# Local and pooled attention in front of a gated MLP: the first six pairs in a short form, weight bits shifted in SBUF, and a new stored order

## The chip, the cores and the metric

The kernel runs on one core of a Trainium2 chip. Its time is device time in microseconds (us). The engines are named as the profile names them: PE (TensorE, matmuls) with PEld (its weight loads), DVE (VectorE), ACT (ScalarE), POOL (GpSimd) and SP (SyncE, which here only starts transfers).

## The reference

For 8 batches and 8 heads, with 576 positions and 64 channels a head, the reference adds two attentions, and passes the joined heads (512 channels) through a gated MLP:

```python
q_d, k_d, v_d = (mean over groups of 4 positions of q, k, v)      # 144 positions
out_up = np.repeat(sm_attn(q_d, k_d, v_d), 4, axis=2)
mask = np.abs(pos[:, None] - pos[None, :]) < 4
scores = np.where(mask, scale * q @ k.T, -1e9)
attn = softmax(scores)                                            # a band of 7
x = out_up + attn @ v                                             # heads joined
h = gelu(x @ w_in); u, v = halves of h                            # 512 -> 1024
v_n = (v - mean) / sqrt(var + 1e-6) * g_ln
gated = u * (w_sg @ v_n + b_sg)                                   # w_sg is 576 x 576
out = x + gated @ w_out
```

All inputs are fp32.

## The kernel before

**Pairs.** Two heads fill the 128 partitions, so there are 32 pairs, g = 0 to 31, four to a batch. Everything is kept transposed (channels or keys on partitions). After the four pairs of a batch comes its MLP. The program is a list of tasks, each with a short name and the pair's number behind it. For a pair:

- `lq`, `lk`, `lv`, `lw` load q, k, v for the pooled part (four rows side by side) and v for the local part; `qs`, `ks`, `vs` sum four neighbours of q, k and v.
- `S` makes the local scores in two PSUM banks (ten tiles of 64 queries by 64 keys: four in one bank, six in the other), `Y` the pooled scores; `YS` is both at once. Of the local tiles only a band counts, so a mask (0 or a large negative number) is added.
- `mx` and `my` take the maxima of rows, `nx` and `ny` make from them the bias of an exponential, `ea` and `eb` are the exponentials of the local tiles (one instruction for each of the ten, since each has a bias of its own; it also gives the sum of its row), `ec` those of the pooled scores; `re` and `rc` make reciprocals, `np` and `nq` normalise.
- `T`, `U`, `t` turn the probabilities with matmuls, `pa`, `pb`, `pc`, `pe` copy them from PSUM; `D` is the product with v, first the pooled part, then the local one; `oe`, `od`, `xa`, `xb` merge both, `xh`, `xl`, `xc` split the result into a high and a low part.

The MLP works on those parts in fp32r, with three products for one (high by high, high by low, low by high): `v` (L691), `u` and `s` and `o` (all L769), with tasks `vg` to `vl`, `ua`, `sa`, `sm`, `gh`, `gl`, `oa` and the store `os` around them.

**Weights.** The weights w_in and w_out come as fp64 words, 512 KB for each of 12 blocks (y0 to y3 for v, z0 to z3 for u, r0 to r3 for o). For each block VectorE or ScalarE scales the high word (`wq`), VectorE shifts its bits into place in two operations (`wb`, L309 and L311; the first writes PSUM), ScalarE scales the low word (`wu`), GpSimd adds (`wt`), and `wh` and `wl` split it into the high and the low part.

**The first four pairs** go another way (`EARLY_S, EARLY_D = 4, 4`). Their mask is added by two matmuls of the identity with the mask ahead of the scores (L417, fp32), and the exponentials read PSUM; the other pairs add the mask on VectorE while copying to SBUF (`ma`, `mb`, L432). And their pooled v is not summed: `D` takes each of the four rows by itself, with 64 pooled matmuls in place of 16 (L573; the local ones are L589).

**What sets the order.** The stored text `ORDER` lists every task once, with the engine behind a slash where there is a choice (`/A`, `/V`, `/P`, for loads `/A` or `/S` is the queue). The program emits the tasks in that order and nothing reorders them later: each engine's queue is the order of its tasks in the text. `place` gives each task its buffer, from 8 PSUM banks and pools of 10 (`X`) and 38 (`R`) SBUF buffers:

```python
SIZES = {"ps": 8, "X": 10, "R": 38}
    order, spots = place(tasks, SIZES)
    with tc.manual_schedule():
        for t, e in order:
            t.emit(e)
```

The mask, the identity, the two turning matrices and g_ln are one array, `small_sb` (463 KB), which SP's queue loads second.

Of the kernel before, what the change touches and what calls it, by code (L numbers as in the profile page):

```python
# [7 lines left out]
F32 = mybir.dt.float32  # L8
# [7 lines left out]
P = 128  # L16
# [72 lines left out]
wy0 lk0/A lq0/A lq1/A small ks0/P wqy0/A wuy0 wby0 wty0 wy3 qs0/V S0 mx0 lw1/A qs1/P nx0/V ea0 why0/V wqy3/V Y0 my0  # L89
lk1/S ks1/P wy1 wuy3 wby3 wqy1/V ny0/A ec0 wly0/P wby1 wty3 wuy1 wty1 wy2 wqy2/A S1 wuy2 wby2 Y1 my1 wty2 lq3 wz2 eb0  # L90
mx1 re0/A rc0 ny1/A ec1 nx1/A ea1 nq0/P lk3 np0/P lk2 wuz2 S3 lq2 S2 wz3 wqz2/V wbz2 mx3 qs3/V lq4 mx2 eb1 wqz3/A T0
pa0/V why3/V U0 t0 pb0/A lv0/S lw0/S nx2/A pc0/V pe0/V ks2/P qs2/P Y2 my2 re1/A rc1 ks3/P ny2/V D0 ea2 eb2 wbz3 qs4/V
wz1 np1/P oe0/V ec2 re2/A nq1/P lk4 ks4/P lv1/S wtz2 od0 xa0 xb0 T1 pa1/A t1 U1 pb1/V pc1/V pe1/A nx3/A Y3 my3 ea3 rc2
np2/P nq2/P wqz1/A ny3/A YS4 xh0/V ma4 mb4 my4 mx4 eb3 ec3 wz0 D1 xl0/P lv2 wbz1 nx4/V T2 lw2 lq5 U2 re3/V oe1/A
wly3/P rc3 np3/P lk5 whz2/A wlz2/P t2 pa2/A wqz0/A pb2/V pc2/V wq3 vk3.0 pe2/A qs5/V ny4/A ec4 D2 wr0 od1 xa1 wuz0
nq3/P wbz0 eb4 T3 vk1.0 lv4 lv3 oe2/V od2 ks5/P xa2 xb2 xb1 lw3 pa3/A wq1 lk6 t3 U3 pb3/V pc3/V wr3 xh1/V why1/A
wly1/V YS5 pe3/A D3 ma5 my5 ea4 re4/A rc4 nq4/V wuz3 lw4 t4 oe3/V wtz0 xl1/P vk3.1 why2/A wly2/P mb5 wr1 xh2/A xl2/V
ks6/V ny5/A mx5 ec5 b lq6 od3 xa3 xb3 xh3/V np4/P xc0 wqr0/A lv5 wur0 wtz3 vk0.0 vk0.1 wq2 xc2 wqr1/A xl3/V nx5/A
# [890 lines left out]
```

## Time and profile before

| | before |
|---|---|
| median of 3 runs | 589.13 us (587.82 to 589.57) |
| span of the profiled execution | 585.7 us |
| PE busy | 559.7 us (96%) |
| PEld busy | 522.2 us (89%) |
| DVE busy | 432.7 us (74%) |
| ACT busy | 354.0 us (60%) |
| POOL busy | 306.2 us (52%) |
| DMA | 63.21 MB, mean 108 GB/s |

The profile shows one execution, from its first instruction to its last (the span); of the profiled execution no other time is given than this span. Shares of busy time are means over the whole span. In what follows, a row of a timeline has a start, a length and the instruction, with the idle time before it and what ended it in brackets; a row of a chain has a start, a length and the work, and "issue" there is time in which an engine waited for nothing that the profile shows; a group of instructions has its line, engine, operation, output and inputs with shape and type, count, then busy us and mean ns, and the idle us before them.

### The profile page before, as it was taken

How to read it: one execution, taken by the hardware profiler on the slowest of the kernel's cores; microseconds unless marked ns; L12 is line 12 of the kernel's file. 1: busy time of each engine (PE TensorE's matmuls, PEld its weight loads, DVE VectorE, ACT ScalarE, POOL GpSimd, SP SyncE). 2: the span in 40 equal slices, each digit the busy share in tenths (PEclk: the TensorE clock that was granted, in tenths of full speed). 3: DMA queues.
4: the chain of work that ended last, by engine and by line, in shares of the span. 5: the costliest groups of instructions: out<-in, count | busy, mean ns of one | idle time of the engine just before them, and what ended most of it. 6: DMA issues, size and time to landing. Idle time of an engine off the chain costs nothing.

```text
span 585.7 us, 17441 instructions
## 1 busy us (share of the span) xinstructions
PE 559.7 (96%) x6992; PEld 522.2 (89%) x6992; DVE 432.7 (74%) x947; ACT 354.0 (60%) x1227; POOL 306.2 (52%) x384
## 2 busy tenths in 40 slices
PE   4778999999999999999999999999999999999997
PEld 2567799988998999989999899988999899998997
DVE  3957998968795998886658786777668877652662
ACT  2958997859868758476656583195833879301300
POOL 4866769674856432461475753554434653820440
PEclk9879999999999999999999999999999999999999
DMA  8999014534503321242046052241117430300103
GB/s 318 305 281 286 14 48 128 158 118 137 144 26 98 97 83 58 96 157 63 16 134 193 13 194 90 59 134 42 37 62 230 118 100 1 113 1 1 41 2 121
DMA packets 30610, 63.21 MB, mean 108 GB/s; under 512 B 3520, under 2 KB 3776, under 8 KB 30528
## 3 DMA queue, kind: packets, MB, share of 16 engines
q1 hardware_dynamic: 29952, 60.86, 33.3%
q8 instruction: 55, 0.90, 0.7%
q10 hardware_dynamic: 576, 1.23, 0.6%
q14 instruction: 27, 0.22, 0.1%
HBM read 52.64 MB, written 9.44 MB: 106 GB/s over the span
## 4 chain that ended last, share of the span: by engine, by line
PE 81%; DVE 8%; ACT 5%; issue 3%; DMA 1%; POOL 0%; SPq 0%; ACTq 0%; DVEq 0%; POOLq 0%
PE ps L769 49%; PE ps L691 15%; PE ps L573 4%; ACT X L484 3%; PE ps L512 3%; PE ps L589 3%; PE ps L424 2%; PE ps L445 2%; PE ps L521 2%; DMA small_sb<-in_small_dram 1%; ACT pd L492 1%; DVE R L740 1%; DVE wsg_l L352 1%; DVE st L721 1%; ACT L492 1%
## 5 line engine op out<-in xcount | busy, mean ns | idle before, releaser
L769 PE MATMUL ps<-wsg_h,R 128*128 128x288 f32 x576 | 120.8, 297 | 0.0
L769 PE MATMUL ps<-R,weight_r 128*128 128x288 f32 x768 | 109.4, 297 | 0.3 <-ACT pd L492 0.3
L769 PE MATMUL ps<-X,weight_z 128*128 128x288 f32 x512 | 108.2, 296 | 0.3 <-DVE X L432 0.3
L769 PEld LDWEIGHTS ps<-R,weight_r 128*128 128x128 f32 x768 | 103.8, 188 | 2.1 <-DVE R L826 0.4
L691 PE MATMUL ps<-weight_y,X 128*128 128x512 f32 x320 | 98.0, 400 | 0.1
L484 ACT ACTIVATE X<-X,nb 128x64 f32<-128x64 f32 x280 | 93.5, 338 | 3.2 <-DVE nb L463 2.8
L769 PEld LDWEIGHTS ps<-wsg_h,R 128*128 128x128 f32 x576 | 94.2, 188 | 0.2
L769 PE MATMUL ps<-wsg_l,R 128*128 128x288 f32 x320 | 92.8, 296 | 0.4 <-DVE wsg_l L352 0.4
L769 PEld LDWEIGHTS ps<-X,weight_z 128*128 128x128 f32 x512 | 83.9, 188 | 1.2 <-ACT weight_z L221 0.7
L769 PE MATMUL ps<-R,weight_z 128*128 128x288 f32 x256 | 75.4, 295 | 0.0
L691 PEld LDWEIGHTS ps<-weight_y,X 128*128 128x128 f32 x320 | 58.2, 189 | 12.5 <-POOL X L221 0.4
L769 PEld LDWEIGHTS ps<-wsg_l,R 128*128 128x128 f32 x320 | 60.2, 188 | 0.6 <-DVE wsg_l L352 0.6
L732 POOL TENSOR_TENSOR rs<-rs,nhalf 128x1 f32<-128x1 f32 (+1 forms) x40 | 24.5, 614 | 63.0 <-DVE rs L723 62.9
L807 DVE SCALAR_TENSOR_TENSOR vs<-ps,small_sb,b_sb 128x288 f32<-128x288 f32 x64 | 32.4, 513 | 32.6 <-PE ps L769 31.6
L484 ACT ACTIVATION_READ_ACCUMULATOR X<-X,nb 128x1 f32 x280 | 53.1, 190 | 0.0
L691 PE MATMUL ps<-weight_y,R 128*128 128x512 f32 x128 | 50.7, 396 | 0.0
L408 POOL TENSOR_TENSOR pairs<-R 112x256 f32<-112x256 f32 x56 | 44.6, 796 | 10.2 <-DMA R<-in_v_dram 10.2
L788 ACT ACTIVATE R<-ps 128x288 f32<-128x288 f32 x64 | 24.7, 411 | 40.9 <-PE ps L769 40.8
L221 ACT CAST R<-R 128x512 fp32r<-128x512 f32 (+2 forms) x44 | 28.0, 641 | 34.0 <-DVE R L814 14.2
L769 PEld LDWEIGHTS ps<-R,weight_z 128*128 128x128 f32 x256 | 48.1, 188 | 0.3
L826 POOL TENSOR_TENSOR R<-R,R 128x576 fp32r<-128x576 f32 x21 | 31.1, 1484 | 28.6 <-PE ps L521 14.4
L814 POOL TENSOR_TENSOR R<-R,vs 128x288 f32<-128x288 f32 x23 | 20.4, 894 | 45.2 <-DVE vs L807 39.2
(111 smaller groups left out, 1210.7 us busy)
## 6 DMA issues: line engine op xcount, KB each, us to landing
R<-in_v_dram SPq DMA_DIRECT2D x56, 224.0 KB, 3.2
X<-in_vw_dram SPq DMA_DIRECT2D x31, 320.0 KB, 4.8
R<-in_kT_dram SPq DMA_DIRECT2D x31, 293.0 KB, 3.8
out_dram<-R SPq DMA_DIRECT2D x31, 288.0 KB, 3.3
R<-in_qT_dram SPq DMA_DIRECT2D x30, 293.0 KB, 4.4
weight_y<-in_w_in_dram SPq DMA_DIRECT2D x4, 512.0 KB, 8.9
weight_z<-in_w_in_dram SPq DMA_DIRECT2D x4, 512.0 KB, 7.9
weight_r<-in_w_out_dram SPq DMA_DIRECT2D x4, 512.0 KB, 6.0
```

The costliest lines, as they stand in the source:

```text
L221: (nc.scalar.copy if e == "A" else ENG[e].tensor_copy)(**kw)
L408: ENG[e].tensor_tensor(out=pairs, in0=v[:, 0:2], in1=v[:, 2:4], op=ALU.add)
L484: nc.scalar.activation(out=st["ms"][:, t, :], in_=src, func=AF.Exp, bias=st["nb"][:, t:t + 1], scale=scale, accum_out=sums[par][:, t:t + 1])
L512: nc.tensor.matmul(out=out, lhsT=st["ms"][0:LD, 2 * c:2 * c + 2, :], rhs=turn_l, is_transpose=True, start=True, stop=True)
L573: nc.tensor.matmul(out=out, lhsT=lhsT, rhs=pdt[ks, probs, h * QC:(h + 1) * QC], start=first, stop=last)
L691: nc.tensor.matmul(out=acc, lhsT=r32(l), rhs=r32(weights[f"y{k}"][:, 0, w]), start=(i == 0 and ks[0] == 0), stop=(i == len(ops) - 1 and ks ...
L732: nc.gpsimd.tensor_tensor(out=rs[0:n], in0=rs[0:n], in1=nhalf[0:n], op=ALU.pow)
L769: nc.tensor.matmul(out=acc[:, 0:HALF], lhsT=r32(l), rhs=r32(r), start=(first and n == 0), stop=(last and n == len(ops) - 1))
L788: nc.scalar.activation(out=us[i // 2][:, half(i)], in_=at["ps", "m", b, "u", i][:, 0:HALF], func=AF.Gelu_apprx_tanh)
L807: nc.vector.scalar_tensor_tensor(out=vsb[i], in0=at["ps", "m", b, "s", i][:, 0:HALF], scalar=g_sb[:, i // 2:i // 2 + 1], in1=b_sb[:, half( ...
L814: ENG[e].tensor_tensor(out=u[:, half(i)], in0=u[:, half(i)], in1=vsb[i], op=ALU.mult)
L826: ENG[e].tensor_tensor(out=r32(gl[d]), in0=us[d], in1=gh[d], op=ALU.subtract)
```

## The change

- **Six pairs, not four, in the short form** (`EARLY, DIRECT = 6, 0`). The mask matmul is now in fp32r: GpSimd rounds the mask and the identity once into a buffer (task `early`). Mask and identity are both stored with the sign turned, so their product is the same.
- **The maximum is taken off in PSUM.** A new task `B` (`below`) multiplies minus the identity with the row maxima, each spread over 64 columns, and adds that to the scores in both banks (two fp32 matmuls). With no bias left that differs from tile to tile, `ea` is one exponential for each bank (128x256 and 128x384), with no sum; `sr`, a VectorE reduction, makes the sums. `nx` and `eb` fall away for these pairs.
- **Pooled v is summed for every pair** (`vs`, on GpSimd or now also VectorE), and `D` has 16 pooled matmuls everywhere. The first four pairs load whole rows of v for it, 0.46 MB where it was 0.39.
- **The shift `wb` stays in SBUF**: the first operation writes the block's SBUF buffer, the second works there in place. It takes no PSUM bank any more.
- **`small_sb` is split** into `early_sb` (mask and minus identity, 295 KB, first on ScalarE's queue) and a smaller `small_sb` (0.18 MB, fifth on SP's).
- **`ORDER` is new from beginning to end**, with other choices of engines: of `pc` 23 of 32 are on ScalarE (before 14), of `xh` 21 (9), of `pb` 20 (15), of `gh` 15 (19); of `xl` 23 are on GpSimd (15), of `qs` 19 (13), of `np` 21 (17); of `vs` 12 are on VectorE (0).

```diff
 ORDER = """
-wy0 lk0/A lq0/A lq1/A small ks0/P wqy0/A wuy0 wby0 wty0 wy3 qs0/V S0 mx0 lw1/A qs1/P nx0/V ea0 why0/V wqy3/V Y0 my0
...
+lq0/S mask/A early/P wy2 lk0/A S0 qs0/P ks0/V Y0 mx0 wqy2/A wby2 wuy2 lv1/A lq1/S qs1/V my0 lk1/S ks1/P small/S B0 ea0
...
         def shift(e):
-            bits, done, hw = like(buf(*keys[1])).bitcast(I32), like(buf(*keys[0])).bitcast(I32), word(1)
-            nc.vector.tensor_scalar(out=bits, in0=hw.bitcast(I32), scalar1=3,
+            done, hw = like(buf(*key)).bitcast(I32), word(1)
+            nc.vector.tensor_scalar(out=done, in0=hw.bitcast(I32), scalar1=3,
                                     scalar2=0x7FFFFFF8, op0=ALU.logical_shift_left, op1=ALU.bitwise_and)
-            nc.vector.scalar_tensor_tensor(out=done, in0=hw.bitcast(I32), scalar=-0x80000000, in1=bits,
+            nc.vector.scalar_tensor_tensor(out=done, in0=hw.bitcast(I32), scalar=-0x80000000, in1=done,
                                            op0=ALU.bitwise_and, op1=ALU.bitwise_or)
...
+        def below(e):
+            for i in range(2):
+                top = bc_last(stats[par][:, i * NA:i * NA + NW[i]], KB)
+                nc.tensor.matmul(out=spv(i), lhsT=minus_sb, rhs=top, start=False, stop=True, skip_group_check=True)
...
+        def exp_early(e):
+            st["ms"] = buf("X", "ms", g).rearrange("p (t k) -> p t k", k=KB)
+            for i in range(2):
+                nc.scalar.activation(out=st["ms"][:, i * NA:i * NA + NW[i]], in_=spv(i), func=AF.Exp, scale=scale)
+
+        def sum_early(e):
+            nc.vector.tensor_reduce(out=sums[par][:, 0:NT], in_=st["ms"], axis=AX.X, op=ALU.add)
...
+            add(N("mx"), {"V": 0.95}, top, [SN(), last_nx])
+            add(N("B"), {"T": 1.2}, below, [N("mx")])
+            add(N("ea"), {"A": 0.75}, exp_early, [N("B")], takes=[("X", "ms", g)],
+                gives=[("ps", "s", g, 0), ("ps", "s", g, 1)], func="e")
+            add(N("sr"), {"V": 0.8}, sum_early, [N("ea"), N("rc", 2)])
```

The rows below are instructions in the order of an engine's queue: line, operation, output and inputs, shape. PE at the very beginning, pair 0, before (mask, scores, then pooled scores; `ps` is a PSUM bank):

```order
L417 MATMUL ps_135<-small_sb 128x256
L417 MATMUL ps_136<-small_sb 128x384
L424 MATMUL ps_135<-R_115,R_117 64x64 x2
L424 MATMUL ps_136<-R_115,R_117 64x64 x2
...
L424 MATMUL ps_136<-R_115,R_117 64x64 x6
L445 MATMUL ps_175<-kd_83,qd_75 64x144 x2
L445 MATMUL ps_176<-kd_83,qd_75 64x144 x2
```

And after (L424 is the mask matmul, L431 the scores, L457 the pooled scores, L438 is `B`; the last two rows are pair 1's pooled scores):

```order
L424 MATMUL ps_123<-R_117 128x256
L424 MATMUL ps_124<-R_117 128x384
L431 MATMUL ps_123<-R_121,R_114 64x64 x2
L431 MATMUL ps_124<-R_121,R_114 64x64 x2
...
L431 MATMUL ps_124<-R_121,R_114 64x64 x6
L457 MATMUL ps_151<-kd_84,qd_76 64x144 x2
L457 MATMUL ps_152<-kd_84,qd_76 64x144 x2
...
L438 MATMUL ps_123<-stats_80,early_sb 128x256
L438 MATMUL ps_124<-stats_80,early_sb 128x384
L457 MATMUL ps_198<-kd_85,qd_77 64x144 x2
L457 MATMUL ps_199<-kd_85,qd_77 64x144 x2
```

The mask matmul reads the rounded buffer, and `B` stands behind the pooled scores of pair 0 and ahead of those of pair 1.

PE at the first `D`, before (L573 pooled with the rows of v in `R`, L589 local):

```order
L573 MATMUL ps_413<-R_386,R_377 64x144 x2
L573 MATMUL ps_414<-R_386,R_377 64x144 x2
...
L573 MATMUL ps_413<-R_386,R_378 64x48 x2
L573 MATMUL ps_414<-R_386,R_378 64x96 x2
...
L589 MATMUL ps_413<-R_364,X_383 64x58 x2
L589 MATMUL ps_414<-R_364,X_383 64x58 x2
```

And after (L589 is now the pooled part with the sums in `vd`, L606 the local part):

```order
L438 MATMUL ps_401<-stats_80,early_sb 128x256
L438 MATMUL ps_402<-stats_80,early_sb 128x384
L589 MATMUL ps_481<-R_374,vd_86 64x144 x2
L589 MATMUL ps_482<-R_374,vd_86 64x144 x2
L589 MATMUL ps_481<-R_374,vd_86 64x48 x2
L589 MATMUL ps_482<-R_374,vd_86 64x96 x2
L606 MATMUL ps_481<-R_315,X_469 64x58 x2
L606 MATMUL ps_482<-R_315,X_469 64x58 x2
```

Of the pooled part a quarter is left, and what stands in front of it is `B` of pair 4, where it was pooled scores.

DVE at its beginning, before (L309 and L311 shift, L391 sums q, L454 is the maximum, L463 the bias, L466 and L468 the pooled maxima):

```order
L309 TENSOR_SCALAR ps_127<-weight_y_113 128x512
L311 SCALAR_TENSOR_TENSOR R_128<-weight_y_113,ps_127 128x512
L391 TENSOR_REDUCE qd_75<-R_117 128x144
L454 TENSOR_REDUCE stats_79<-ps_135 128x4
L454 TENSOR_REDUCE stats_79<-ps_136 128x6
L463 TENSOR_SCALAR nb_90<-stats_79 128x10
...
L466 TENSOR_REDUCE stats_79<-ps_175 128x2
L468 TENSOR_REDUCE stats_79<-ps_176 128x1
L309 TENSOR_SCALAR ps_195<-weight_y_132 128x512
L311 SCALAR_TENSOR_TENSOR R_196<-weight_y_132,ps_195 128x512
```

And after (L315 and L317 shift, L397 sums, L466 is the maximum, L478 and L480 the pooled maxima, L503 is `sr`; the rows left out between are pooled sums of q and a bias):

```order
L397 TENSOR_REDUCE kd_84<-R_121 128x144
L466 TENSOR_REDUCE stats_80<-ps_123 128x4
L466 TENSOR_REDUCE stats_80<-ps_124 128x6
L315 TENSOR_SCALAR R_164<-weight_y_119 128x512
L317 SCALAR_TENSOR_TENSOR R_164<-weight_y_119,R_164 128x512
...
L478 TENSOR_REDUCE stats_81<-ps_198 128x2
L480 TENSOR_REDUCE stats_81<-ps_199 128x1
L503 TENSOR_REDUCE sums_82<-X_185 128x10
L466 TENSOR_REDUCE stats_81<-ps_212 128x4
L466 TENSOR_REDUCE stats_81<-ps_213 128x6
...
L315 TENSOR_SCALAR R_262<-weight_z_259 128x512
L317 SCALAR_TENSOR_TENSOR R_262<-weight_z_259,R_262 128x512
```

The first shift has moved behind the first maximum, the second (of block z2) behind the maxima of pairs 1 and 2, and pair 0's `sr` stands between the pooled and the local maxima of pair 1.

More of the change, by code (lines that the diff above doesn't have):

```diff
@@ L94 @@
[L94 to L98, printed above, removed]
@@ L273 @@
         nc.vector.memset(t.rearrange("p (b k) -> p b k", k=KB)[:, :, QC:KB], 0.0)
[L276 removed]
+    add("mask", {"S": 0.5, "A": 0.5}, lambda e: DQ[e].dma_start(out=early_sb, in_=masks), mb=0.3)
+    add("small", {"S": 0.5, "A": 0.5}, lambda e: DQ[e].dma_start(out=small_sb, in_=small), mb=0.17)
     add("b", {"S": 0.5}, lambda e: nc.sync.dma_start(out=b_sb, in_=b_sg.broadcast_to([P, S])), mb=0.3)
+    add("early", {"A": 0.6, "V": 0.4, "P": 1.3}, lambda e: copy(e, out=r32(buf("R", "early")[:, 0:7 * KB + P]), in_=early_sb), ["mask"],
+        takes=[("R", "early")])
     weights = {}
@@ L285, in weight64 @@
         shape = [P, src.shape[1], 2, src.shape[2] // 2]
-        keys = ("R", "w", t), ("ps", "b", t)
+        key = "R", "w", t
         def like(ap):
@@ L317, in total @@
         def total(e):
-            done = like(at[keys[0]]).bitcast(I32)
+            done = like(at[key]).bitcast(I32)
             nc.gpsimd.tensor_tensor(out=done, in0=done, in1=word(0).bitcast(I32), op=ALU.add)
@@ L330, in weight64 @@
         add(f"wq{t}", {"A": 0.56, "V": 0.7}, scaled, [f"w{t}"])
-        add(f"wb{t}", {"V": 1.42}, shift, [f"wq{t}"], takes=keys, gives=keys[1:])
+        add(f"wb{t}", {"V": 1.42}, shift, [f"wq{t}"], takes=[key])
         add(f"wt{t}", {"P": 1.3}, total, [f"wb{t}", f"wu{t}"])
         add(f"wh{t}", {"A": 0.56, "V": 0.4}, high, [f"wt{t}"])
-        add(f"wl{t}", {"P": 1.3, "V": 0.66}, low, [f"wh{t}"], gives=keys[:1])
+        add(f"wl{t}", {"P": 1.3, "V": 0.66}, low, [f"wh{t}"], gives=[key])
     for k in range(KT):
@@ L380, in load_v4 @@
             for i in range(2):
-                for rows in (slice(0, QC), slice(HD, QD)) if early_d else (slice(0, QD),):
+                for rows in (slice(0, QC), slice(HD, QD)) if direct else (slice(0, QD),):
                     DQ[e].dma_start(out=st["v4"][i][rows], in_=v4[b, p, i, rows].rearrange("j (f d) -> j f d", f=FAC))
@@ L564, in av @@
             o = [buf("ps", "o", g, i) for i in range(2)]
-            pdt, fs = st["pdt"], range(FAC if early_d else 1)
+            pdt, fs = st["pdt"], range(FAC if direct else 1)
             def pooled(i, h, f, t, cols, probs):
                 ks, hs = slice(i * KB, i * KB + QC), slice(h * HD, (h + 1) * HD)
-                lhsT = st["v4"][t][ks, f, hs] if early_d else st["vd"][ks, t, hs]
-                first, last = t == 0 and f == 0, t == 1 and f == fs[-1]
                 c0 = NTP * QB + cols.start * QC
                 out = o[i][hs, c0:c0 + (cols.stop - cols.start) * QC].rearrange("p (i m) -> p i m", m=QC)
-                nc.tensor.matmul(out=out, lhsT=lhsT, rhs=pdt[ks, probs, h * QC:(h + 1) * QC], start=first, stop=last)
+                lhsT = st["v4"][t][ks, f, hs] if direct else st["vd"][ks, t, hs]
+                nc.tensor.matmul(out=out, lhsT=lhsT, rhs=pdt[ks, probs, h * QC:(h + 1) * QC],
+                                 start=t == 0 and f == 0, stop=t == 1 and f == fs[-1])
             for f in fs:
@@ L954, in _layout @@
     m = np.stack([first, band, band, band, band, band, last], axis=1)
-    mask = np.where(m, 0.0, NEG).astype(np.float32)
+    mask = np.where(m, 0.0, -NEG).astype(np.float32)
     g = inputs["moe_g_ln"].reshape(KT, P).T
```

277 lines of the change are left out of this document (141 added, 136 removed).

## The prediction

> **What bounds the kernel now.** I read the stretches of the profile first, then the chain that ended last, then the timeline of the engine that the chain names most beside TensorE, and last the groups of instructions for prices. The stretches, with the columns start:end, length, busy time of PE, PEld, DVE, ACT and POOL (instructions), granted clock, DMA share and GB/s:
>
> ```profile
> 0.00:60.00 60.00, 41.70 (x830) 33.65 (x831) 39.20 (x92) 39.23 (x178) 39.39 (x51) 0.89 0.92 293
> 60.00:100.00 40.00, 39.31 (x363) 36.52 (x363) 37.57 (x71) 36.95 (x101) 29.48 (x32) 1.00 0.20 60
> 100.00:570.00 470.00, 466.89 (x5714) 440.48 (x5713) 351.45 (x776) 277.87 (x949) 235.91 (x303) 1.00 0.29 88
> ...
> 10.00:30.00 20.00, 16.13 (x304) 11.62 (x304) 16.57 (x38) 16.46 (x90) 15.60 (x19) 0.90 1.00 325
> 30.00:45.00 15.00, 11.51 (x240) 10.42 (x237) 8.86 (x23) 8.65 (x41) 10.00 (x10) 0.73 0.96 292
> 45.00:60.00 15.00, 12.61 (x295) 10.44 (x295) 11.24 (x26) 11.61 (x46) 10.26 (x13) 0.95 0.86 264
> ```
>
> From 100 to 570 us PE stands still for 470 − 466.89 = 3.1 us: there the time is PE's work, and nothing taken off another engine can win more than that. The first 60 us are different: PE is idle for 18.3 us, the clock is 0.73 in one part, the DMA engines are full (0.96 to 1.00 from 10 to 45 us), and VectorE, ScalarE and GpSimd are each busy for about 39 of 60 us. The change acts in this head. The chain in it (start, length, what):
>
> ```profile
> 1.18 7.32 DMA small_sb<-in_small_dram
> 8.54 2.50 PE ps L417 x4
> 11.04 1.07 PE ps L424 x30
> 12.14 0.93 DVE stats L454 x2
> ...
> 26.62 3.25 PE ps L573 x49
> ...
> 37.30 3.11 issue
> 40.41 0.56 PE ps L573 x6
> ...
> 45.84 1.90 PE ps L573 x55
> 47.90 0.52 PE ps L589 x26
> ...
> 52.30 2.05 issue
> 54.34 1.38 PE ps L573 x42
> ```
>
> The pooled matmuls of D (L573) stand on it four times, with two stretches in the middle of them in which PE waited for no semaphore. The DVE's idle time behind these four D, in its timeline (start, length, instruction, in brackets the idle time before it):
>
> ```profile
> 31.27 0.31 DVE L556 TENSOR_SCALAR da<-ps 128x144 f32<-128x144 f32 x1 [1.65 <-PE ps L589]
> 44.19 0.64 DVE L221 COPY R<-ps 128x116 f32<-128x116 f32 x2 [4.07 <-PE ps L521]
> 48.45 0.31 DVE L556 TENSOR_SCALAR da<-ps 128x144 f32<-128x144 f32 x1 [0.77 <-PE ps L589]
> 56.51 0.31 DVE L556 TENSOR_SCALAR da<-ps 128x144 f32<-128x144 f32 x1 [2.72 <-PE ps L589]
> ```
>
> So VectorE, the engine that has the most to do between 10 and 30 us, stood still for 1.65 + 4.07 + 0.77 + 2.72 = 9.2 us because PE was in a D of the long form.
>
> **The change part by part.** *Pooled v summed for the first four pairs too.* D of pairs 0 to 3 loses 48 of 64 pooled matmuls. Later pairs show the short form:
>
> ```profile
> 102.19 0.56 PE ps L573 x15
> 102.75 0.53 PE ps L589 x34
> ```
>
> That is 1.1 us for a whole D, where the third, the shortest of the four, lasted 2.6 (45.84 to 48.42) and the first 4.6, to VectorE's operation at 31.27; two hold the stalls of 3.11 + 2.05 = 5.2. PE has 18 us of idle time there already, so its own gain counts little; what counts is the 9.2 us in which VectorE waited for it. What is late next is the sum vs in front of D: three of the first four run on GpSimd, one on VectorE.
>
> ```profile
> L408 POOL TENSOR_TENSOR pairs<-R 112x256 f32<-112x256 f32 x56 | 44.6, 796 | 10.2 <-DMA R<-in_v_dram 10.2
> L409 POOL TENSOR_TENSOR vd<-pairs 112x128 f32<-112x128 f32 x56 | 27.7, 494 | 4.4
> ```
>
> One vs is 2 x 0.80 + 2 x 0.49 = 2.6 us on GpSimd (about half on VectorE, an estimate from 128x640 reductions at 0.81). Its loads carry 0.46 MB instead of 0.39 per pair, on a full DMA; since D waits for v, vw and the probabilities anyway, and GpSimd has 20 us free in the head, I cost the load and the sums on GpSimd at nothing; without that cover each D would come 2.6 us later. Behind a short D VectorE may still wait as it did behind the third, 0.77, four times 3.1. That leaves 9.2 − 3.1 = 6.1 to come back: **−6.1**, between 0 (VectorE waits as long for something else) and −9.2.
>
> *The two stalls.* The DMA queues of 37 to 41 us (packets, MB, share of the engines):
>
> ```profile
> q1 hardware_dynamic: 628, 1.09, 105.6%
> q8 instruction: 1, 0.02, 1.5%
> ```
>
> A packet of instructions comes in behind a full data queue just inside the first stall, and PE runs on after it. I read the stalls as PE running out of code in a burst of very short matmuls. 192 matmuls less, and as many weight loads, make that burst shorter. The Trainium skill, page "Runtime: NRT & Kernel Launch", section "Instruction fetch mechanics", says that a fetch of the next block is mostly hidden. By that rule these 5.2 us would have another cause and could stay; no run yet shows which.
>
> *Masks, maxima and exponentials.* Prices:
>
> ```profile
> L484 ACT ACTIVATE X<-ps,nb 128x64 f32<-128x64 f32 x40 | 12.0, 326 | 6.3 <-DVE nb L463 6.2
> L484 ACT ACTIVATION_READ_ACCUMULATOR X<-ps,nb 128x1 f32 x40 | 8.8, 219 | 0.0
> L788 ACT ACTIVATE R<-ps 128x288 f32<-128x288 f32 x64 | 24.7, 411 | 40.9 <-PE ps L769 40.8
> L456 DVE TENSOR_REDUCE stats<-X 128x10 f32<-128x640 f32 x28 | 22.8, 813 | 0.5
> L432 DVE TENSOR_TENSOR X<-ps,small_sb 128x256 f32<-128x256 f32 x28 | 11.6, 416 | 4.8 <-PE ps L424 4.6
> L432 DVE TENSOR_TENSOR X<-ps,small_sb 128x384 f32<-128x384 f32 x28 | 15.3, 547 | 0.0
> L417 PE MATMUL ps<-small_sb 128*128 128x256 f32 x8 | 3.3, 502 | 8.5 <-DMA small_sb<-in_small_dram 8.5
> L417 PE MATMUL ps<-small_sb 128*128 128x384 f32 x8 | 4.1, 602 | 0.3 <-DVE R L311 0.3
> ```
>
> The local exponentials of a pair are 1.20 + 1.77 = about 3 us in the chain now; in two pieces, priced by a 128x288 one, 0.39 + 0.49 = 0.9. ScalarE gains some 2 us in each of six pairs, less a few copies that it takes over from VectorE. ScalarE is 16.46 of 20 us busy between 10 and 30 us, so part of this can reach the chain, but it then waits for the matmul B behind the maximum, and B is priced by L417, which is also plain fp32 of 128x256 and 128x384: (3.3 + 4.1) / 4 = 1.85 us a pair, 2.50 the first. The mask matmul in front of the scores becomes fp32r, at 0.3 (an estimate from 128x288 matmuls of that type, 297 ns). PE's cost for both is 4 x (1.85 + 0.3 − 1.85) + 2 x 2.15 = 5.5 us, and lies in PE's idle 18.3 us. At the start, the keys of pair 0 go second on ScalarE's queue, where two queries now land:
>
> ```profile
> R<-in_qT_dram ACTq DMA_DIRECT2D x2, 293.0 KB, 8.4
> ```
>
> With 0.4 to the issue they are there at 8.8, and 8.8 + 0.3 + 1.07 + 0.93 + 1.85 = 13.0 us is when the exponentials can begin, now 13.41. I take **−0.5**, between −2.5 (B wholly covered) and +1.85 (B on top of everything).
>
> VectorE loses the two mask additions of pairs 4 and 5, 2 x 0.96 = 1.9 us in all, and gets one sum over 640 elements for each of six pairs, 6 x 0.813 = 4.9.
>
> *The shift in SBUF.* Before, it goes through PSUM:
>
> ```profile
> L309 DVE TENSOR_SCALAR ps<-weight_z 128x512 int32<-128x512 int32 x4 | 2.8, 689 | 0.3 <-ACT pd L492 0.3
> L311 DVE SCALAR_TENSOR_TENSOR R<-weight_z,ps 128x512 int32<-128x512 int32 x4 | 2.7, 686 | 0.1
> L305 DVE TENSOR_SCALAR weight_y<-weight_y 128x512 f32<-128x512 f32 x2 | 0.8, 417 | 0.0
> L740 DVE TENSOR_SCALAR R<-R,mv,rs 128x512 f32<-128x512 f32 x32 | 20.8, 654 | 2.8 <-POOL rs L732 2.7
> ```
>
> An operation of that size wholly in SBUF took 0.417 us (L305), so the first of the two may win 0.27, twelve times 3.2. But L740, equally in SBUF, has a mean of 0.654 instead, 0.24 above: twelve times 2.8 lost. Ends −3.2 and +2.8; I take 0, the middle, both rows being equally near. The Trainium skill, page "SBUF — State Buffer", section "Who interferes with whom", speaks against this part: a VectorE operation with two SBUF inputs and a GpSimd one that reads SBUF shut each other out, and so does a two-port one. The trace agrees so far as L740 can be long and L309 and L311, with an operand in PSUM, are not. By that rule the part would cost up to the 2.8 us just named.
>
> *The order.* Through the new order VectorE also takes over weight and key work and hands copies from PSUM to ScalarE. Counted over the stored order up to the end of pair 3's merge, each kind at its mean, VectorE has 43.6 us of work before and 45.2 after: +4.9 for sums, −1.0 for one pair's mask additions fewer (two pairs before, one after), −1.4 for one shift fewer, −0.9 for all the rest. This is **+1.6**, between 0 (it fits where VectorE was idle) and +4.9 (the sums alone, nothing handed off). Behind 60 us PE's work falls in neither kernel on anything that the change takes away; I cost the reordering there and the tail at 0, ±0.5.
>
> **The sum** −6.1 − 0.5 + 1.6 = −5.0, so a span of 585.7 − 5.0 = 580.7. The span is of one profiled execution; the median of the runs, 589.13, lies 3.4 above it. That gives 584.1 us.
>
> **The rivals.** *The stalls stay.* If PE's two stretches of 5.2 us have another cause, only 6.1 − 5.2 = 0.9 comes back: −0.9 − 0.5 + 1.6 = +0.2, a median of 589.3, within 0.3% of before (1.8 us, about what a measurement of this kernel can tell from no change). For it: PE waits for no semaphore there, and the DMA is full after the change as well. Against it: the packet in the stall, and the third D, which ran without one, is the shortest.
>
> *VectorE bounds the head, and gets longer.* The chain of a pair gets two more hops: maximum on VectorE, B on PE, exponential on ScalarE, and back to VectorE for the sum, where before the exponentials delivered it themselves. VectorE's queue is in order: a sum that waits for its exponential holds up pooled sums, shifts and merges behind it. If VectorE's idle time moves there, nothing of the 9.2 comes back, and +1.6 to +4.9 stays: 591 to 594, decided once less than 2 us of the 9.2 come back. For it: 16.57 of 20 us busy between 10 and 30. Against it: 6.1 and 3.8 us idle in the two windows after that, enough to take the sums in.
>
> *More than the sum.* All 9.2 come back and B is covered: −9.2 − 2.5 + 1.6 = −10.1, a median of 579.0. For it: ScalarE, 16.46 of 20 us busy, loses some 2 us a pair. Against it: the first D needs its loads in any case, and the DMA share is 1.00.
>
> **How the numbers follow.** The forecast, a head shorter by 1.8 to 13 us, has a chance of 0.62, with the case of more in it; stalls that stay, or any other way to within 0.3%, 0.17; VectorE's longer queue, or a reordered middle in which PE has 3.1 us to win and more to lose, 0.21. The likeliest is 584.1, and its own range 576 to 587.4. The lower end is −10.1 with the shift's −3.2, 575.8; the upper, to leave no more than 2 in 10 out, takes in the same and the smaller half of the slower case, 592.
>
> **What would show it.** Right: D of pairs 0 to 3 at about 1.1 us each; no idle time of VectorE over 1 us behind them; no stall of PE above 2 us inside D; PE's busy share of 0 to 60 us nearer to 50 than to 42 at equal work, so that the first long run of L769 (88.35 us now) is met some 5 us earlier; B at 1.85 us a pair, exponentials at 0.4 to 0.5 each, sums at 0.81. Wrong: stalls of the same length in other bursts, VectorE waiting for L500 in front of the sums, GpSimd's vs as the releaser of D, shifts of 0.9 us and more, or PE idle time beyond 3.1 us after 100 us.

## The result: 608.2 us, 3.4% slower

The changed kernel took 608.17 us (median of 4 runs, 605.01 to 611.05), beside 588.48 us for the kernel before in the same session: a ratio of 1.0342, with a 95% interval of 1.0288 to 1.0396. The prediction was 584.1 us, with a range of 576 to 592: wrong in sign. The profiled span is 609.3 us, 23.6 more than before. (Two runs below, before_one_input and before_gate_from_psum, had three executions each over 1.5% above the fastest of the same kernel; their medians and ratios leave these out.)

The stretches of the profile after, in the columns of the prediction's first fence, and the page's shares of the chain that ended last by engine (before: PE 81%, DVE 8%):

```profile
0.00:60.00 60.00, 44.72 (x737) 34.48 (x738) 51.15 (x94) 41.20 (x140) 44.27 (x57) 0.94 1.00 303
60.00:100.00 40.00, 37.34 (x531) 33.99 (x530) 38.08 (x74) 29.65 (x87) 34.10 (x41) 0.96 0.50 153
100.00:570.00 470.00, 456.77 (x5291) 425.67 (x5290) 348.37 (x758) 261.04 (x893) 231.58 (x272) 0.98 0.25 78
```

```profile
PE 66%; DVE 20%; ACT 4%; POOL 4%; issue 4%; DMA 2%; SPq 0%; ACTq 0%; DVEq 0%; POOLq 0%
```

The head did become better for PE: it is busy for 44.7 of 60 us (before 41.7). To compare two orders, I priced the matmuls that both kernels have (without the masks, B and the pooled part of D, which the change replaces) at their median distance to the next in the trace of before: at 60 us the changed kernel has done 17.8 us of such work and the kernel before 13.0, a lead of 4.8. But VectorE is busy for 51.2 of the 60 us (39.2), and the lead is gone at about 91 us; at 100 us PE is about 3 us behind, and between 100 and 570 us PE stands still for 13.2 us where it stood for 3.1. What PE waits for from 60 to 600 us (engine, line, what, us in total, times, longest):

```profile
PE ps L538 <- DVE pd L526: 3.6, 1, 3.6
PE ps L589 <- ACT R L223: 2.9, 1, 2.9
PE ps L538 <- DVE vs L828: 2.2, 1, 2.2
PE ps L790 <- DVE R L781: 2.0, 2, 1.3
PE ps L790 <- DVE R L613: 1.0, 1, 1.0
```

VectorE is behind most of these, though over the whole span it is only 75% busy. The three longest are paid for twice. The first of them, and the stretch right behind it, in the columns of the first fence:

```profile
161.50:164.30 2.80, 0.05 (x1) 0.00 (x0) 2.80 (x3) 0.00 (x0) 2.80 (x3) 1.00 1.00 375
164.40:171.10 6.70, 5.95 (x27) 5.95 (x28) 3.33 (x7) 3.63 (x12) 3.38 (x7) 0.50 1.00 345
```

From the last microsecond of the wait on, PE's granted clock is 0.50 for 6.8 us. Between 60 and 570 us there are four such stretches of 3.4 or 6.8 us, at 92.7, 164.4, 256.5 and 318.0 us, 20.5 us in all, each in or right behind waits of PE that add up to 1.6 us or more; the kernel before has none there. From 60 to 570 us PE thus stands still for 12.1 us more than before, and the lower clock costs about 10 more (an estimate: half of 20.5). Together that is 22 of the 28.4 us that are lost behind the head's lead.

How VectorE loses time shows where one normalising of pooled probabilities (L526, 0.60 us at its shortest) takes 3.93. VectorE's timeline there, and then GpSimd's:

```profile
30.48 0.45 DVE L613 TENSOR_TENSOR R<-ps,od 128x290 f32<-128x290 f32 x1
30.84 3.93 DVE L526 TENSOR_TENSOR pd<-pd,rc 128x432 f32<-128x432 f32 x1
34.70 0.45 DVE L613 TENSOR_TENSOR R<-ps,od 128x290 f32<-128x290 f32 x1
```

```profile
30.79 0.45 POOL L415 TENSOR_TENSOR vd<-pairs 112x128 f32<-112x128 f32 x1
31.20 1.27 POOL L325 TENSOR_TENSOR R<-R,weight_y 128x512 int32<-128x512 int32 x1
32.44 1.25 POOL L523 TENSOR_TENSOR X<-X,rc 128x640 f32<-128x640 f32 x1
33.65 0.66 POOL L400 TENSOR_TENSOR half<-R 128x288 f32<-128x288 f32 x1
34.39 0.67 POOL L401 TENSOR_TENSOR kd<-half 128x144 f32<-128x144 f32 x1
```

The operation has both inputs in SBUF. GpSimd was at work when it was issued, it was not done while three more operations of GpSimd ran behind that one, and ended 0.46 us after the fourth, which ended at 34.31. The operations with an operand in PSUM around it (L613) have their usual 0.45. I call *held time* what an operation of VectorE takes beyond the 10th percentile of its kind and shape in both kernels together. (So a shift through PSUM, at 0.69 us, counts 0.27 although nothing holds it.) Over the kernel it is 46 us before and 78 after; the part of it that lies on the chain is 7.4 us before and 33.8 after. These 26 us are about the 23.6 between the spans. That the two agree is a hint and not a proof, since the chain shows one path and not what else would have been late; the runs with one input below are the test.

### The profile page after: what moved, and what is told of

The parts are those of the page before. It is cut to its first block, busy times and chain, and to the rows that moved or that the text cites. A ratio compares the mean times of both kernels' runs of the same rounds, so it can differ in the third digit from the quotient of the medians.

```text
span 609.3 us, 17009 instructions
## 1 busy us (share of the span) xinstructions
PE 574.7 (94%) x6820; PEld 529.5 (87%) x6820; DVE 457.2 (75%) x959; ACT 335.8 (55%) x1127; POOL 318.3 (52%) x376
## 4 chain that ended last, share of the span: by engine, by line
PE 66%; DVE 20%; ACT 4%; POOL 4%; issue 4%; DMA 2%; SPq 0%; ACTq 0%; DVEq 0%; POOLq 0%
PE ps L790 41%; PE ps L712 13%; PE ps L589 2%; PE ps L606 2%; PE ps L457 2%; PE ps L529 2%; PE ps L538 2%; PE ps L431 2%; DVE pd L526 1%; DVE pairs L414 1%; DVE R L761 1%; DMA R<-in_v_dram 1%; ACT X L493 1%; DVE vd L415 1%; DVE R L781 1%
## 5 line engine op out<-in xcount | busy, mean ns | idle before, releaser
L790 PE MATMUL ps<-wsg_h,R 128*128 128x288 f32 x576 | 127.8, 308 | 4.4 <-DVE R L781 2.0
L790 PE MATMUL ps<-X,weight_z 128*128 128x288 f32 x512 | 112.4, 301 | 0.0
L790 PEld LDWEIGHTS ps<-wsg_h,R 128*128 128x128 f32 x576 | 97.1, 195 | 6.9 <-DVE R L781 2.5
L790 PE MATMUL ps<-wsg_l,R 128*128 128x288 f32 x320 | 95.0, 302 | 0.9 <-DVE wsg_l L358 0.9
L493 ACT ACTIVATE X<-X,nb 128x64 f32<-128x64 f32 x260 | 86.9, 338 | 1.4 <-DVE nb L475 1.0
L625 POOL TENSOR_TENSOR R<-R,X 128x576 fp32r<-128x576 f32 x23 | 35.2, 1534 | 37.4 <-DVE X L223 16.1
L493 ACT ACTIVATION_READ_ACCUMULATOR X<-X,nb 128x1 f32 x260 | 49.3, 190 | 0.0
L223 ACT COPY R<-ps 112x288 f32<-112x288 f32 (+4 forms) x88 | 32.1, 401 | 26.6 <-PE ps L538 9.1
L864 DVE TENSOR_TENSOR R<-ps,R 128x288 f32<-128x288 f32 x64 | 27.6, 448 | 22.6 <-PE ps L790 22.4
L781 POOL TENSOR_TENSOR R<-R,R 128x512 fp32r<-128x512 f32 (+1 forms) x21 | 28.5, 1364 | 30.4 <-ACT R L223 10.6
```

What stands on the lines that cost most here:

```text
L223: (nc.scalar.copy if e == "A" else ENG[e].tensor_copy)(**kw)
L493: nc.scalar.activation(out=st["ms"][:, t, :], in_=st["ms"][:, t, :], func=AF.Exp, bias=st["nb"][:, t:t + 1], scale=scale, accum_out=sums[p ...
L625: ENG[e].tensor_tensor(out=r32(st["xl"]), in0=st["x"][:, 0:S], in1=st["xh"][:, 0:S], op=ALU.subtract)
L781: ENG[e].tensor_tensor(out=r32(dst), in0=vact[s][0][0:n], in1=vh[0:n, 0:DM], op=ALU.subtract)
L790: nc.tensor.matmul(out=acc[:, 0:HALF], lhsT=r32(l), rhs=r32(r), start=(first and n == 0), stop=(last and n == len(ops) - 1))
L864: nc.vector.tensor_tensor(out=x[:, half(i)], in0=at["ps", "m", b, "o", i][:, 0:HALF], in1=x[:, half(i)], op=ALU.add)
```

## Experiments

Each ratio is to the kernel before in the same session (its medians there: 585.6 to 586.8 us).

**The parts of the change, each alone in the kernel before.** First the shift:

```diff
-nc.vector.tensor_scalar(out=bits, ...)                      # bits in PSUM
-nc.vector.scalar_tensor_tensor(out=done, ..., in1=bits, ...)
+nc.vector.tensor_scalar(out=done, ...)                      # done in SBUF
+nc.vector.scalar_tensor_tensor(out=done, ..., in1=done, ...)
```

> The kernel before, with one edit: the first shift of the weight bits writes the SBUF buffer and the second works there in place; order and engines are those of before. Theory H (held): an operation of VectorE whose operands are all in SBUF is held while GpSimd works, as the traces show for 24 shifts of the changed kernel (L315 and L317 up to 1.7 and 1.8 us, where L309 and L311 took 0.69). Then the 24 shifts here have a mean above 0.75 us and the kernel is slower, by 1 to 6 us. Theory O (order): the time is lost by the new stored order behind 60 us, and the shift is worth nothing by itself: within 1.8 us of before, the first shifts at about 0.42 us.

588.8 us, ratio 1.0070 (1.0034 to 1.0106): 4.1 us slower by the ratio, as H said, and the 24 operations have a mean of 0.95 us. Two shifts in its VectorE timeline, with GpSimd's beside them:

```profile
15.82 1.40 DVE L309 TENSOR_SCALAR R<-weight_y 128x512 int32<-128x512 int32 x1
17.26 0.69 DVE L311 SCALAR_TENSOR_TENSOR R<-weight_y,R 128x512 int32<-128x512 int32 x1
17.87 0.42 DVE L309 TENSOR_SCALAR R<-weight_y 128x512 int32<-128x512 int32 x1
18.32 1.66 DVE L311 SCALAR_TENSOR_TENSOR R<-weight_y,R 128x512 int32<-128x512 int32 x1
```

```profile
15.58 1.36 POOL L319 TENSOR_TENSOR R<-R,weight_y 128x512 int32<-128x512 int32 x1 [1.14 <-ACT pd L492]
18.09 1.34 POOL L319 TENSOR_TENSOR R<-R,weight_y 128x512 int32<-128x512 int32 x1 [1.14 <-DVE R L311]
```

Not held by GpSimd, the first operation takes 0.42 (in PSUM 0.69) and the second 0.69. Issued while GpSimd's L319 runs, each waits for its end (16.94 and 19.43) and finishes about 0.3 and 0.55 us behind it. The first has one tensor as its input, and is held all the same.

The pooled sums, on GpSimd and then on VectorE:

```diff
-EARLY_S, EARLY_D = 4, 4
+EARLY_S, EARLY_D = 4, 0
 ORDER: +vs0 ahead of D0, +vs1 behind nq2, +vs2 ahead of D2, +vs3 ahead of D3   (all /P, or all /V)
```

> The kernel before, with one edit: v of pairs 0 to 3 is summed on GpSimd ahead of their D (four tasks put into the stored order: ahead of D0, behind nq2, ahead of D2 and of D3), and D has 16 pooled matmuls. The prediction's step: 6.1 us of VectorE's waits come back, 583 us. Its rival (the two stalls of PE stay, with another cause): 589. If the sums on GpSimd are late, D waits for them instead: up to 2.6 us per pair, 590 to 595. H and O say nothing of this one, since nothing is added on VectorE and the order stays.

> As sums_alone (the kernel before, v of pairs 0 to 3 summed ahead of D, 16 pooled matmuls, the same four places in the order), but the four sums are on VectorE. There the sums on GpSimd stood on the chain (D0 waited for them until 28.8 us) and pushed the normalising of the next pairs back. Theory G (GpSimd's in-order queue took what D gave back): VectorE, idle for 9.2 us around these D, takes 1.4 us for a sum, so 3 to 6 us come back, 580 to 583 against a before of 585.6. Theory N (the long D was cover for other waits, loads and ScalarE, and was worth nothing): 584 to 587. If VectorE is held by GpSimd in the sums (two inputs in SBUF), 1.4 becomes 2 to 3 us a sum and the gain is at most 2 us.

On GpSimd 587.5 us, 1.0052 (1.0023 to 1.0082); on VectorE 592.9, 1.0108 (1.0073 to 1.0144). Both are slower, against the prediction's step and against G. What PE waits for between 25 and 62 us, in the kernel before, with the sums on GpSimd, and with the sums on VectorE (the longest row of each):

```profile
PE ps L573 <- issue: 5.2, 2, 3.1
```

```profile
PE ps L572 <- POOL vd L408: 8.2, 6, 3.3
```

```profile
PE ps L572 <- DVE vd L408: 11.2, 6, 3.4
```

And the chain in front of the first D, with the sums on GpSimd:

```profile
26.35 0.69 POOL pairs L407
27.11 0.45 POOL vd L408
27.56 0.69 POOL pairs L407
28.33 0.46 POOL vd L408
28.83 0.57 PE ps L572 x7
```

D0 is short, and ends only 0.9 us sooner (30.49 us, before 31.41): its matmuls begin 2.2 us later than the 26.62 of before. On VectorE the four sums are held like the shifts (10.7 us of held time in the first 60 us, before 3.9).

The short form of masks, maxima and exponentials, for the first four pairs:

```diff
-mx, nx, ea (4 exponentials), eb (6)      # a bias and a sum for each tile
+mx, B, ea (one exponential a bank), sr   # B behind mx, sr where eb was
```

> The kernel before, with the short form of masks, maxima and exponentials for its first four pairs (mask matmul in fp32r, B behind mx, one exponential a bank, sr where the second exponentials stood; the mask array loaded apart and first of the two), and nothing else: D of the first pairs long, shift through PSUM, order and engines of before. The prediction's terms: -0.5 at the start, about 2 us of ScalarE freed a pair, +3.2 us of sums on VectorE, which has idle time behind D. P (these terms): 584 to 586. Q (the extra hops from VectorE to PE to ScalarE and back, each with its wait, lengthen each pair's chain in an order that was made without them): 588 to 594.

589.0 us, 1.0107 (1.0062 to 1.0153): Q. The extra hop shows in a wait of PE, in front of a B:

```profile
PE ps L438 <- DVE stats L466: 4.2, 1, 4.2
```

So none of the three parts made that kernel faster by itself.

**The order.** The changed kernel with the first 250, and the first 345, words of its order, then all else in the old order:

> The changed kernel with the first 250 words of its stored order (through the merge and split of pair 3, to about 55 us), and behind them all other tasks in the order and with the engines of before; all edits stay in. O: the head's gain (at 60 us PE is 4.8 us ahead of before) stays and nothing is lost behind it: 582 to 586 us. H: eight of the twelve shifts and one sum on VectorE are in this head, which is as it was, but the other eleven sums on VectorE are back on GpSimd, so H too expects most of the loss to be gone: 584 to 592. Neither would be right with 600 or more, which would say that the head leaves the rest of the program something behind (late loads, late weights).

> The changed kernel with the first 345 words of its stored order (to about 85 us, the last of the weights y and z prepared) and all other tasks in the order and with the engines of before. At 80 us PE is 3.4 us ahead of before in the changed kernel, at 90 us 0.8. O (the new order behind 85 us loses the rest, 16 us): 584 to 589. E (the edits lose it, whatever the order: held operations, late loads): 600 or more. In new_head_old_rest the loss came at 60 to 80 us, where u of batch 0 waited for the block z1, whose shift the old order places earlier; that doesn't arise here.

594.7 us, 1.0189 (1.0139 to 1.0240): neither O nor H. And 600.7 us, 1.0241 (1.0205 to 1.0277): not O, and E's number. What PE waits for, the first kernel from 60 to 600 us, the second from 25 to 600 (the longest rows):

```profile
PE ps L429 <- issue: 3.5, 1, 3.5
PE ps L710 <- POOL X L221: 3.1, 1, 3.1
PE ps L788 <- POOL weight_z L330: 2.4, 1, 2.4
```

```profile
PE ps L788 <- POOL weight_z L330: 8.0, 1, 8.0
PE ps L536 <- DVE pd L524: 3.5, 1, 3.5
```

PE's lead of the head meets work on weights that is not done yet: the old order asks for u, which needs the z weights, sooner than the new head has them ready. I read this as a lead that is in part bought with weight work put off; no run separates that. The switch of orders makes the 8.0 us wait by itself, so the second run's time doesn't show E's reason, and the two runs don't divide the loss between the stretches.

> The changed kernel, with the 12 of 32 sums of pooled v that it has on VectorE put on GpSimd at the same places of the order. H: these 48 operations (28.5 us on VectorE, with two inputs in SBUF, single ones held to 1.4 and 1.7 us) stand ahead of PE's waits at 160, 250 and 447 us: 8 to 14 us come back, 594 to 600. O: the places in the order are what is wrong, and GpSimd takes 2.6 us for a sum where VectorE takes 1.4 when it isn't held: 606 to 614.

605.9 us, 1.0371 (1.0306 to 1.0436), no different from the changed kernel's 1.0342: H expected more, and the time lies just below O's range. GpSimd takes 2.4 us for what VectorE did, and PE then waits for GpSimd's queue too:

```profile
PE ps L536 <- DVE pd L524: 4.7, 1, 4.7
...
PE ps L455 <- POOL kd L399: 2.3, 1, 2.3
```

> The changed kernel in its own new order throughout, but from word 251 on each task is on the engine that it had before (325 words changed, among them all sums of v from vs4 on to GpSimd). V (the choice of engines makes the loss, since VectorE gets more operations between SBUF buffers that GpSimd holds up): 588 to 596. O (the order of the tasks makes it): 602 or more, since the new order was made for its own engines.

641.6 us, 1.0949 (1.0912 to 1.0985): as O expected, not the choice of engines by itself. The new order belongs to its engines.

**Held time, taken away.** Every VectorE addition, product and difference of two SBUF tensors becomes a reduction of one input and the same length, in both kernels. That leaves the second operand out of the computation, so these kernels measure time and are no replacement:

```diff
-ENG["V"].tensor_tensor(out=out, in0=a, in1=b, op=op)
+nc.vector.tensor_reduce(out=out, in_=(b if op is a difference else a)[..., None], axis=AX.X, op=ALU.add)
```

> The kernel before, in which every VectorE addition, product and difference of two SBUF tensors (normalising, sums of v, low parts, gating) is replaced by a reduction over a last axis of length 1, which reads one of the two and writes the same output: it leaves the second operand out of the computation, at the same length (640 elements 0.81 us in both forms). H: with one input they aren't held; of 7.4 us of held time on this kernel's chain 2 to 5 go, 580 to 585 against 586. O: no change.

> The same replacement in the changed kernel, order and engines its own (the shifts of weights and the scaling of the layernorm stay as they are). Read along the chain, held time of VectorE is 33.8 us in the changed kernel and 7.4 before, 26 us more, against 23.6 us between the two spans. H: most of that goes, 588 to 596, and the distance to before_one_input is under 12 us. O (what is late is late by the order, and held time only fills waits that would be there anyway): 602 to 609, a distance of 18 or more.

Before: 582.6 us, 0.9942 (0.9901 to 0.9983). After: 584.1 us, 0.9973 (0.9936 to 1.0011). The changed kernel loses its whole handicap, 3.4% become nothing that can be told, and the distance between the two kernels shrinks from 20 us to 1.5. H, and by more than it asked. The normalising and the two additions of a sum of v, first in the changed kernel, then in it with one input:

```profile
L526 DVE TENSOR_TENSOR pd<-pd,rc 128x432 f32<-128x432 f32 x19 | 19.5, 1032 | 0.3
L414 DVE TENSOR_TENSOR pairs<-R 112x256 f32<-112x256 f32 x24 | 14.9, 622 | 0.0
...
L415 DVE TENSOR_TENSOR vd<-pairs 112x128 f32<-112x128 f32 x24 | 13.6, 566 | 1.1 <-PE ps L589 0.2
```

```profile
L231 DVE TENSOR_REDUCE pd<-pd 128x432 f32<-128x432 f32 x19 | 10.9, 577 | 0.0
L231 DVE TENSOR_REDUCE pairs<-R 112x256 f32<-112x256 f32 x24 | 9.8, 408 | 0.0
...
L231 DVE TENSOR_REDUCE vd<-pairs 112x128 f32<-112x128 f32 x24 | 6.9, 286 | 1.8 <-PE ps L602 1.0
```

0.577, 0.408 and 0.286 us on average, where the shortest with two inputs were 0.60, 0.40 and 0.29: GpSimd is busy beside them (45.3 of the first 60 us), and none of the three kinds shows held time. The stretches of that kernel:

```profile
0.00:60.00 60.00, 47.70 (x808) 36.15 (x809) 51.71 (x102) 44.31 (x144) 45.28 (x63) 1.00 1.00 308
60.00:100.00 40.00, 40.00 (x627) 37.96 (x626) 35.49 (x90) 35.47 (x128) 33.18 (x41) 1.00 0.55 165
100.00:570.00 470.00, 466.82 (x5330) 438.05 (x5329) 324.55 (x761) 255.25 (x856) 214.75 (x274) 1.00 0.25 78
```

PE stands still for 3.2 us between 100 and 570, as before the change (3.1), does not wait at all from 60 to 100, and the granted clock is 1.00 throughout. So neither the new order nor the short form loses by itself: with the same order and engines nothing is lost once these operations aren't held. The values don't lift the clock: before_one_input has 0.89 in the first 60 us, as the kernel before.

Two things go along with it. GpSimd gains as well: it is busy for 293.2 us with one input and for 318.3 in the changed kernel, so the run takes the waits of both engines away and doesn't say whose cost more. And an operand that is not read any more can let its buffer go sooner; no run separates that. Not all held time is gone: counted as above, 39 of 78 us are left, about half of them in the shifts and in the scaling of the layernorm (both stay as they are), but only about 2 us lie on the chain.

**The shift in the new order.** Ten of twelve shifts through PSUM again, without and with the one-input form:

> The changed kernel in its own order and with its own engines, but ten of the twelve shifts go through a PSUM bank as before (blocks y0 and z1, where no bank is free, stay in SBUF). H (operations between SBUF buffers are held by GpSimd): these 20 operations are back at 0.69 us with no spread, VectorE's held time in the first 60 us (11.3 us in the changed kernel, 3.9 before) falls by 3 to 5, and with it 2 to 6 us of the time: 602 to 606 where the changed kernel has 608. O (order): no change, 606 to 610.

> Both: the replacement by one input, and ten of twelve shifts through PSUM. H: another 2 to 5 us less than after_one_input, 584 to 592; and the stretch from 60 to 100 us, where PE loses 10.7 us in the changed kernel and 3.1 before, loses under 6. O: as after_one_input, 602 or more.

610.9 us, 1.0441 (1.0395 to 1.0488), and 587.4 us, 1.0027 (0.9990 to 1.0063). H fails here: held time in the first 60 us does fall, from 11.3 to 8.1 us, but the time does not: the ratio is 1% higher than the changed kernel's. With one input all around, the SBUF form is the better one by 3.3 us in the medians (the intervals overlap a little), although its two operations take 0.93 and 1.02 us there on average and 0.69 each through PSUM. PE's waits say what the PSUM form costs. In the run without the one-input form:

```profile
PE ps L426 <- DVE R L319: 1.7, 2, 1.1
PE ps L531 <- DVE R L319: 1.7, 1, 1.7
PE ps L714 <- DVE R L319: 1.0, 1, 1.0
```

L319 is the second operation of the shift, whose result none of these matmuls reads: behind it the shift's PSUM bank comes free. With two smaller rows PE waits 5.4 us for it, with one input 5.1, and not at all in the two kernels whose shifts stay in SBUF. So it is the bank, and not the length of the shift, that the SBUF form wins in the new order, as I read it.

**Which operations, in forms that compute the same.** Sums of v by one reduction over the four rows; then also the gating with its second operand left in PSUM:

```diff
+nc.vector.tensor_reduce(out=vd[:, i], in_=v.rearrange("p f d -> p d f"), axis=AX.X, op=ALU.add)
...
-vsb[i] = vs2[i % 2]
+vsb[i] = at["ps", "m", b, "s", i][:, 0:HALF]       # 36 of 39 on VectorE; 38 of 41 in the kernel before
```

> The changed kernel, in which the twelve sums of v on VectorE are one reduction over the four rows for each half (one input, 112x128 from 112x512) in place of two additions of two inputs each. H: 11.7 us of the 77 us of held time were in these 48 additions, and several stand in PE's chain (157 to 159, 250 to 253, 443 to 446 us): 5 to 12 us come back, 596 to 603. If moving them to GpSimd brought nothing because they are not what counts: 606 to 610.

> As after_sums_one_input, and for 36 of the 39 gatings on VectorE the result of L828 stays in its PSUM bank until the gating reads it there, which leaves that product one input in SBUF. 7.8 us of held time were in the gatings: another 2 to 5 us, 592 to 600.

604.9 us, 1.0313 (1.0273 to 1.0352), and 600.5 us, 1.0255 (1.0218 to 1.0292). The first is 0.3% less than the changed kernel, inside the intervals and less than H asked; both together are 0.9% less, half a us above what was expected, and the intervals just touch. By subtraction the rest of the 3.4% would be in the other kinds (normalising, low parts of the splits), which no run took away alone.

> As sums_alone_on_vector (the kernel before, v of pairs 0 to 3 summed on VectorE ahead of D, 16 pooled matmuls), but with the one-input sum. There PE waited 11.2 us for the sums, and the time was 6 us over before. H (they were held): the sums take 0.6 to 0.7 us a half and never more, 584 to 588. N (D waits for loads and for VectorE's queue whatever the sum takes): 590 to 593. The prediction's 583 would need that D's wait were VectorE's only one.

587.1 us, 1.0019 (0.9990 to 1.0047), 0.9% less than with the held sums: H, though a half took 1.04 us and not 0.6 to 0.7. PE's wait for the sums falls from 11.2 to:

```profile
PE ps L575 <- DVE vd L407: 6.7, 5, 2.5
```

> The kernel before, in which 38 of the 41 gatings on VectorE read the bias sum from its PSUM bank (as in after_sums_and_gate). 9.1 us of its 46 us of held time were in these, 7.4 of all of it on the chain: 0.5 to 2.5 us come back, 583.5 to 585.5 against 586. If the banks held longer make PE wait for a bank: 587 to 590.

588.2 us, 1.0011 (0.9974 to 1.0047): no change that can be told, where some was expected. There is no version here that computes the same and beats the kernel before.

## Why the prediction was wrong

- **"I cost the reordering there and the tail at 0, ±0.5."** This step carried most of the error. Behind 60 us the changed kernel lost a lead of 4.8 us and, by the spans, 23.6 more: PE stood still for 12.1 us more, and ran for 20.5 us at half the clock. The prediction looked behind 60 us for work that the change removes, and not for what new neighbours do to work that stays. Its list of signs of being wrong had this one (PE idle beyond 3.1 us after 100 us), and its chance of 0.21 covered a middle with "more to lose", but no term of the sum gave that a price.
- **VectorE's +1.6.** It priced each kind at the mean that it had in the kernel before. That mean holds the waits of one order: the normalising on VectorE has 0.806 us before, 1.032 after and 0.577 with one input. VectorE was busy for 12 us more in the head, of which 7.4 are held time.
- **The shift at 0, "the middle".** Alone it costs 4.1 us, above the upper end of 2.8. The row of L740 pointed there and was put at the middle. And the term counted the first operation only: in shift_alone that has 0.79 us on average (0.69 through PSUM), but the second, which now has two inputs in SBUF, 1.11 (0.69), twelve times 0.42 more.
- **The sums, −6.1.** Against the sum's largest term, by the ratios +3.0 us on GpSimd, +6.3 on VectorE, and +1.1 (no change that can be told) on VectorE without held time. The step that failed is "GpSimd has 20 us free in the head, I cost the load and the sums on GpSimd at nothing". Free time in an in-order queue is not free where D needs it: PE now waits 8.2 us for POOL, and VectorE still waits 9.0 us for PE between 25 and 62 us (before 9.6). With the sums on VectorE its own waits for PE do go (1.5 us), and PE waits 11.2 us for VectorE. "Without that cover each D would come 2.6 us later" is what happened, to within 0.4 for D0.
- **The two stalls.** With D short the 5.2 us of "issue" are gone from D, as the prediction read them, but the changed kernel has one of 2.0 us, in the local part of a D (a row of PE's waits from 10 to 62 us):

```profile
PE ps L606 <- issue: 2.0, 1, 2.0
```

 Counted along PE's matmuls, the stalls of before stand behind numbers 467 and 717, and in early_form_alone behind 469 and 720; in the changed kernel this one stands behind 718, in other work. A place in the stream of instructions, 250 apart, fits blocks of code that come late. No run shows that cause. The rival of stalls that stay had its half of the truth, without deciding anything.
- **The small prices held, the −0.5 did not.** Groups of the changed kernel up to 70 us:

```profile
L438 PE MATMUL ps<-stats,early_sb 128*128 128x384 f32 x12 | 4.9, 493 | 0.0
L438 PE MATMUL ps<-stats,early_sb 128*128 128x256 f32 x12 | 4.4, 454 | 1.0 <-DVE stats L466 1.0
L500 ACT ACTIVATE X<-ps 128x384 f32<-128x384 f32 x6 | 3.0, 502 | 0.3 <-PE ps L438 0.3
L503 DVE TENSOR_REDUCE sums<-X 128x10 f32<-128x640 f32 x6 | 4.8, 797 | 0.0
```

 B is (4.9 + 4.4) / 6 = 1.55 us a pair (1.85), the larger exponential 0.50 (0.49), sr 0.80 (0.81); the masks cost 0.87 a pair and not 0.3, since the row behind that is one matmul and a pair has two. These prices were not the trouble. But the −0.5, between −2.5 and +1.85, is not borne out: in four pairs of the kernel before the short form cost 1.07%, 6.3 us, VectorE's sums included. That is in an order made without it, and how much of it stays in the new order is open.
- **The rival "VectorE bounds the head, and gets longer"** named the engine and the sign, with a share in the 0.21, but sized it at 591 to 594 and put it down to the extra hops, for which only early_form_alone speaks. What makes VectorE longer in the changed kernel is held time, and most of it falls behind the head: of the 31 us more, 7.4 up to 60 us, 3.5 to 100 and 20.5 behind.
- **The page's rule.** By the Trainium skill, page "SBUF — State Buffer", section "Who interferes with whom", a VectorE operation with two SBUF inputs and a GpSimd operation that reads SBUF shut each other out. The runs agree (3.93 us in place of 0.60; with one input the normalising takes at most 0.60). The prediction applied it to the 24 operations of the shift only; it bears as much on every operation of that kind whose neighbours the new order changes.

## What to carry to other kernels

Before a reorder, count on each side the operations that share something with another engine: their mean time is a property of the order, not of the operation, and only the shortest of a kind is its price. An idle share does not make an engine with an in-order queue free; ask where in its queue the new work stands, and who needs it there. Where two engines lock each other out, look for a form that escapes the lock, here a reduction or an operand left in PSUM, before moving the work to another engine; the forms that compute the same won back at most 0.9% here. And a wait of PE of two us or more can cost a slow stretch behind it too.

## What the runs showed of the hardware

A held VectorE operation does not get its turn behind the one GpSimd instruction that it met: three more ran ahead of it (30.84 to 34.77 us). A reduction over a last axis of length 1 costs no more than the two-input form at its shortest (0.577 to 0.60 us at 128x432), and is not held; one input alone is not enough, since the shift of one SBUF tensor was held to 1.40 us (0.42). And in or right behind pauses of PE of 2.0 to 3.6 us its granted clock fell to 0.50 for 3.4 or 6.8 us (those from 161.6, 252.8 and 315.8 us of the changed kernel on, and the two stalls of the kernel before). Not behind each one: a pause of 2.9 us in after_sums_and_gate, from 160.9 us on, had no such stretch.
